# Attention into two expert layers on one core: the first set's tokens split by parity, items of two head pairs, and earlier loads

## The chip, the cores and the metric

One NeuronCore of one Trainium2 chip runs the whole program. The metric is the device time of one execution in microseconds. Five engines work side by side, each through its own queue in program order: TensorE (PE in the rows, its weight loads are PEld), VectorE (DVE), ScalarE (ACT), GpSimd (POOL) and SyncE (SP, which issues most of the DMAs).

## The reference

Three stages, all in float32. The tokens of all four sequences together are 2304, in rows of 512 features (8 heads of 64).

```python
# q, k, v: (4, 8, 576, 64); attention inside chunks of 64 tokens
scores = scale * q_c @ k_c.T            # per chunk and head
attn = softmax(scores)                  # sum + 1e-9 below the fraction line
x = (attn @ v_c) as rows (2304, 512)
p = domain_probs / (sum + 1e-9)         # 4 experts
x = sum over e of p[:, e] * (relu(x @ w1[e]) @ w2[e])      # 512 -> 1024 -> 512
h = x @ w_in                            # 512 -> 2048
out = (h * clip(h + 3, 0, 6) / 6) @ w_out                  # -> 512
```

## The kernel before

Every product of the two expert layers is made of three TensorE passes over a high and a low part of both operands (`HL`). The tokens are three sets of 768, each set two halves (z) of N = 384. The hidden features come in groups of 512: eight groups in phase 0 (4 experts), four in phase 1. Group 0 of a set is done plainly (`h_plain`, line 789). Every other group makes its four blocks of h from seven products of sums and differences of operands (`h_pair`, line 743), which `build_x` (lines 523 to 530) makes on ACT and DVE from the set's tokens. `y_unit` (line 836) multiplies the gated h by the second weight, and `finish` adds it up.

The order of work is written by a planner (`Plan`). Each piece of work is an `op` with an engine, an assumed duration, a due time, buffers and, for some, a time before which it may not start (`hold`). `Plan.run` plays them through once, in Python. `Plan.emit` then issues them in that order, and so each engine's queue has a fixed order on the chip. TensorE's products of the layers are the main list and keep their order. The attention's small TensorE steps are side work, put between them. While nothing is ready for TensorE early on, `fill` (line 249) issues a product of the identity with itself: one of 128 columns wherever the plan is between 3 and 40 us and sees TensorE free.

Set 0 is the start of the program. Its group 0 is cut into three parts of 256 tokens, and each part has two items (`Item`), an item being 128 tokens by all four head pairs. An item runs: load q, k, v (line 331, all from SP's queue, packets of 256 B), transpose q and k on TensorE (376), copy them out (480), scores (387), maximum, subtraction, exponential, sum and reciprocal (401 to 432), the weighing by it (436, on DVE in the first part and on POOL in the others), transpose the probabilities (440), copy (443), values (449), and two copies into the set's token tile `xs` (462). `build_plain` then makes the high part (559, ACT) and the low part (560, DVE) of the part's tokens, and `h_plain` of the part, 48 products of 256 columns, and its y, 24 products of 512 columns, can go. The two halves z are the first and the second 32 tokens of each chunk. Items of sets 1 and 2 are one head pair by 384 tokens and transpose on DVE (381).

The first group's weights come as one 1 MB load (`rh`, line 589). ACT casts each of its four quarters to the high part (582), POOL subtracts to the low part (583). They are also stored to DRAM for the later sets (`keep`, line 576). In SBUF, the identity (512 B a partition) stands ahead of the tile of all x operands (`x7`), then small constants and a pad, then the weight tiles `wh` and `wy` and the gated `gt`.

Of the kernel before, what the change touches and what calls it, by code (L numbers as in the profile page):

```python
# [21 lines left out]
PAD = 32  # L22
# [25 lines left out]
class Plan:  # L48
# [3 lines left out]
    LAT = 0.2  # L52

# [16 lines left out]
    def run(self):  # L70
# [51 lines left out]
        fillers = []  # L122

# [9 lines left out]
        while done < len(self.ops):  # L133
# [19 lines left out]
            for e in ready:  # L153
# [34 lines left out]
ANY = {"t", "a", "y", "h", "cm", "rh", "wp", "s", "w64", "tx"}  # L188
# [3 lines left out]
def fused_kernel(ctx: ExitStack, tc: tile.TileContext, q, k, v, probs, w1, w2, win, wout, out):  # L192
# [26 lines left out]
    x7 = const.tile([P, 7, 2, 2, N], F32R, name="x7")  # L219
# [4 lines left out]
    pn = const.tile([P, NT // P, NE], F32, name="pn")  # L224
    prs = const.tile([P, NT // P], F32, name="prs")

    const.tile([P, PAD], F32, name="pad")
    own = {tag: pool(tag, 1) for tag in ("wh", "wy", "gt")}
    sb = pool("sb", 1)
# [21 lines left out]
    plan = Plan({tag: n for tag, (n, _, _) in SHAPES.items()}, filler, 40.0)  # L251
# [85 lines left out]
    class Item:  # L337


        def __init__(self, si, ps, c0, n, by_pe=False, tags={}):  # L340
# [10 lines left out]
            self.xs = xs_of((0, si))  # L351

        def flat(self, b):
            return b.t.bitcast(F32).rearrange("p f w -> p (f w)") if b.tag in ("w64", "wp") else b.t
# [9 lines left out]
        def load(self, b, src, natural):  # L364
            if natural:
                h0 = 2 * self.ps[0]
                load_nat(self.nat(b), src, h0, h0 + 2 * len(self.ps), self.t0, self.n)
            else:
                w = 2 * self.nm
                t = b.t[:, :self.nc_ * 96].rearrange("p (c k) -> p c k", k=96)  # L370
                for i, p in enumerate(self.ps):
                    load_qk_t(t[:, i * w:(i + 1) * w], src, p, self.t0, self.n)

        def turn_pe(self, b, ps):
            for u in range(self.nu):
                nc.tensor.transpose(ps.t[:, u * P:(u + 1) * P], self.rows(b, u).rearrange("p h d -> p (h d)"), ident)  # L376

        def turn_dve(self, b, o, r):
            t = b.t[:, :self.nc_ * 96].rearrange("p (c k) -> p c k", k=96)
            d = o.t[:, :self.cols].rearrange("p (c i r) -> p c r i", c=self.nc_, r=2)  # L380
            nc.vector.transpose(out=d[:, :, r, :], in_=t[:, :, 64 * r:64 * r + 32])

        def scores(self):
            for c in range(self.nc_):
                for h in range(2):
# [3 lines left out]
                        self.flat(self.qT)[a, c * CH:(c + 1) * CH],  # L389
# [66 lines left out]
        def leave(self, c):  # L456
# [4 lines left out]
            d = d[:, 0] if len(self.ps) == 1 else d[:, :, 0]  # L461
            nc.scalar.copy(d, src)

        def place(self, t, step, quick=False, banks="aay"):
# [3 lines left out]
            ahead = 12.0  # L468
            by = self.by_pe
            for n_, (tag, src) in enumerate((("qr", q), ("kr", k), ("vr", v))):  # L470
                b, nat = getattr(self, tag), by or tag == "vr"
                kb = self.cols * P * 4 / 1000 * (1 if nat else 1.5)
                o[tag] = op("SP", 0.3, lambda b=b, src=src, nat=nat: self.load(b, src, nat), due(0 if n_ < 2 else 2) - ahead, new=[b], lag=kb / 200, hold=max(due(0) - 40, 0))
            for j, (a, z) in enumerate((("qr", "qT"), ("kr", "kT"))):
                src, dst = getattr(self, a), getattr(self, z)
                if by:
                    ps = buf("y")
                    x = op("PE", self.nu * 0.11, lambda src=src, ps=ps: self.turn_pe(src, ps), due(0), [o[a]], [ps], [src], side=True)
                    e_ = "ACT" if z == "qT" or not quick else "DVE"
                    f = (lambda dst=dst, ps=ps: nc.scalar.copy(self.flat(dst)[:, :self.cols], ps.t[:, :self.cols])) if e_ == "ACT" else (lambda dst=dst, ps=ps: nc.vector.tensor_copy(self.flat(dst)[:, :self.cols], ps.t[:, :self.cols]))  # L480
                    o[z] = op(e_, (act if e_ == "ACT" else dve)(self.cols), f, due(0), [x], [dst], [ps])
# [3 lines left out]
            self.psS, self.psP, self.px = buf(banks[0]), buf(banks[1]), [buf(banks[1]), buf(banks[2])]  # L485
            s = op("PE", self.nc_ * 0.036, self.scores, due(1), [o["qT"], o["kT"]], [self.psS, self.e], [self.qT, self.kT], side=True)
            if by:
# [8 lines left out]
            g = quick  # L496
            x = op("DVE" if g else "POOL", (dve if g else gps)(self.cols), lambda: self.weigh(nc.vector if g else nc.gpsimd), due(2) + 1, [x], (), [self.e, self.sm])
            x = op("PE", self.nu * 0.11, self.turn_p, due(3), [x], [self.psP, self.pT], [self.e], side=True)
            x = op("ACT", act(self.cols), self.copy_p, due(3), [x], (), [self.pT, self.psP])
            born = self.xs.born  # L500
            x = op("PE", self.nu * 0.22, self.values, due(4), [x, o["vr"], born], [*self.px, *([] if born else [self.xs])], [self.vr, self.pT, self.xs], side=True)
# [44 lines left out]
    def build_plain(key, c0, n, after, due):  # L546
# [3 lines left out]
        for d, z in [(d, zs) for zs in ((slice(0, 2),) if n < N else (slice(0, 1), slice(1, 2))) for d in range(2)]:  # L550
# [22 lines left out]
    def keep(ph, g, name, b, after, due):  # L573

        D = kept[ph, g, name] = dpool.tile([P, 2, 512], F32R, name=f"k{len(kept)}")
        stored[ph, g, name] = op("SP", 0.5, lambda: nc.sync.dma_start(out=raw(D), in_=raw(b.t)), due, after, (), [b], lag=1.75)

    def split_w(b, src, after, due, new, use, halves=True):
# [4 lines left out]
        return op("POOL", gps(512), lambda: nc.gpsimd.tensor_tensor(out=view(b.t[:, 1]), in0=read(), in1=raw(view(b.t[:, 0])), op=ALU.subtract), due, [hi, *after], (), [b, *use])  # L583
# [40 lines left out]
    def weights(ph, si, g):  # L624
# [17 lines left out]
        else:  # L642
            R, ld = load_h(ph, g, 1.0, 0)
            for d, f in ((0, 0), (1, 0), (0, 1), (1, 1)):
                b = wo[key, d, f] = buf("wh")
                x = wready[key, d, f] = split_w(b, lambda d=d, f=f: R.t[:, 2 * d:2 * d + 2, 256 * f:256 * f + 256], [ld], 6.0 + d + 2 * f, True, [R])
                keep(ph, g, (d, f), b, [x], 40)
        e, h = divmod(g, HS)
        for n_, f in enumerate(FO):
# [3 lines left out]
            ld = op("SP", 0.5, lambda Y=Y, r0=r0: nc.sync.dma_start(out=Y.t, in_=w2[e, r0:r0 + P, :]), (t_y - 8 if g else 2.0) + n_, (), [Y], lag=1.0, hold=hold_y)  # L653
            x = wready[key, "y", f] = split_w(b, lambda Y=Y: Y.t, [ld], t_y + 2 * n_, True, [Y], False)
            keep(ph, g, f, b, [x], t_y + 2 * n_ + 3)
# [121 lines left out]
    def h_plain(u, f, zs):  # L777
# [3 lines left out]
        ps = buf("h")  # L781
# [3 lines left out]
        def fn():  # L785
            for k_ in range(4):
# [7 lines left out]
        deps = [*(wready[key, d, f // 2] for d in range(2)), *(xplain[si, c0, d, z] for d in range(2) for z in zs)]  # L794
        x = op("PE", 12 * mm(m), fn, t, deps, [ps], [*Ws, *Xs])
# [49 lines left out]
    def out_rows(si, z, j):  # L845
        r0 = si * ST + 2 * P * j
        return out[r0:r0 + 2 * P, :].rearrange("(c z q) d -> z c q d", z=2, q=Q)[z]
# [59 lines left out]
    def domain_load():  # L907
        rows = probs.rearrange("(r c z q) e -> z c q r e", c=4, z=2, q=Q)
        d = pr.rearrange("p (r z) e -> p r z e", z=2)
        for z in range(2):  # L910
            for c in range(4):
                nc.sync.dma_start(out=d[32 * c:32 * c + 32, :, z, :], in_=rows[z, c])
# [11 lines left out]
    op("PE", 0.23, filler, 100, (), (), [warm], side=True, hold=40.3)  # L924

    SPARE = [{}, {"qr": "w64", "kr": "w64", "qT": "wp", "kT": "wp", "pT": "t"}]
    first_set = []
    for i in range(2 * N // PART):
        t = 3.0 + 11 * i
        after = []  # L930
# [81 lines left out]
```

## Time and profile before

| | |
|---|---|
| median of 3 runs | 1233.15 us (1231.62 to 1235.03) |
| the profiled execution | 1233.94 us, span 1232.2 us |
| mean granted TensorE clock | 0.997 |
| TensorE busy | 1213.1 us, 98% of the span |
| VectorE, ScalarE, GpSimd busy | 702.4, 515.1, 495.7 us |

The profiled execution lies 0.79 us above the median, and 1.74 us of it are outside the span. A busy TensorE includes products that only fill time (line 249) and products that run at the lower clock, so the 98% says little by itself about what could be saved. The rows below are of the profiled execution. Times in them are microseconds from the start of the span unless marked ns.

### The profile page before, as it was taken

The page shows a single profiled execution, that of the slowest core. Times are in us where ns is not written, and L with a number is a line of the kernel's source. Part 1 is how long each engine was busy: PE and PEld are TensorE (multiplying, and loading weights), DVE is VectorE, ACT ScalarE, POOL GpSimd, SP SyncE. Part 2 cuts the span into 40 slices and gives each one's busy share as a digit, 9 for nine tenths or more (in the row PEclk, how much of TensorE's full clock was granted, in tenths as well). Part 3 has the DMA queues.
Part 4 walks back from the last instruction along what each step waited for, and adds up shares of the span by engine and source line. Part 5 has one row for each costly group of instructions (what it writes and reads, how often), then busy time and mean ns, then how long its engine had stood idle before and what let it go on. Part 6 is the DMA issues. An engine that isn't in the chain of part 4 may idle for free.

```text
span 1232.2 us, 19532 instructions
## 1 busy us (share of the span) xinstructions
PE 1213.1 (98%) x7196; PEld 1090.1 (88%) x7196; DVE 702.4 (57%) x1267; ACT 515.1 (42%) x1149; POOL 495.7 (40%) x565
## 2 busy tenths in 40 slices
PE   9999999999999999999999999999999999999997
PEld 8888888888988888899998999998999999999996
DVE  4355645546634676557736655546455845584554
ACT  4554545454344455434453443324423442243221
POOL 3456655563244655455465574511111111111110
PEclk9999999999999999999999999999999999999999
DMA  8868877748679889878778878858555865675552
GB/s 241 283 223 290 275 233 264 254 191 284 209 211 316 264 269 281 273 267 262 223 258 273 288 269 293 300 188 259 186 185 186 269 205 188 188 239 188 188 171 52
DMA packets 150639, 292.32 MB, mean 237 GB/s; under 512 B 71056, under 2 KB 80528, under 8 KB 150160
## 3 DMA queue, kind: packets, MB, share of 16 engines
q0 software_dynamic: 43488, 158.35, 40.1%
q1 hardware_dynamic: 106864, 132.58, 33.2%
q8 instruction: 57, 0.93, 0.3%
q14 instruction: 38, 0.31, 0.1%
q10 hardware_dynamic: 192, 0.13, 0.0%
HBM read 213.95 MB, written 77.07 MB: 236 GB/s over the span
## 4 chain that ended last, share of the span: by engine, by line
PE 88%; POOL 3%; issue 3%; DMA 3%; SPq 2%; DVE 1%; ACT 1%; DVEq 0%; POOLq 0%; ACTq 0%
PE y L836 44%; PE h L743 35%; PE h L789 4%; PE y L249 1%; PE a L387 1%; SPq L324 1%; POOL wh L583 1%; DMA qr<-in_q_dram 1%; DMA rh<-in_moe_w_dram 1%; PE a L895 1%; PE a L449 1%; DMA w<-in_moe_w_in_dram 1%; POOL t L609 1%; PE y L376 0%; PE a L440 0%
## 5 line engine op out<-in xcount | busy, mean ns | idle before, releaser
L836 PE MATMUL y<-wy,gt 128*128 128x512 f32 x2592 | 606.6, 392 | 2.8 <-DVE gt L811 2.6
L836 PEld LDWEIGHTS y<-wy,gt 128*128 128x128 f32 x2592 | 484.3, 188 | 102.8 <-DVE gt L811 3.1
L743 PE MATMUL h<-x,wh 128*128 128x384 f32 x2772 | 500.1, 339 | 3.2 <-DVE c L753 1.6
L743 PEld LDWEIGHTS h<-x,wh 128*128 128x128 f32 x2772 | 485.6, 188 | 8.7 <-DVE c L753 3.2
L634 POOL DMA_DIRECT2D wh<-k x190 | 103.1, 543 | 210.0 <-PE h L743 198.9
L753 DVE TENSOR_TENSOR c<-h,c 128x384 f32<-128x384 f32 x264 | 145.8, 552 | 72.6 <-PE h L743 68.7
L637 POOL DMA_DIRECT2D wy<-k x112 | 61.6, 550 | 267.1 <-PE y L836 259.6
L863 DVE SCALAR_TENSOR_TENSOR acc<-y,pn,acc 128x512 f32<-128x512 f32 x126 | 88.6, 750 | 120.1 <-PE y L836 120.1
L753 DVE TENSOR_TENSOR c<-h,p 128x384 f32<-128x384 f32 x66 | 36.7, 556 | 137.2 <-PE h L743 118.2
L808 DVE TENSOR_TENSOR gt<-c,gt 128x384 fp32r<-128x384 f32 x126 | 97.4, 777 | 16.7 <-ACT gt L807 16.4
L760 ACT COPY p<-h 128x384 f32<-128x384 f32 x66 | 31.4, 476 | 175.1 <-PE h L743 175.1
L806 ACT ACTIVATE c<-c 128x384 f32<-128x384 f32 x126 | 65.5, 525 | 77.5 <-DVE c L753 77.2
L870 DVE TENSOR_TENSOR acc<-y,acc 128x512 f32<-128x512 f32 x53 | 36.3, 691 | 65.2 <-PE y L836 65.2
L807 ACT CAST gt<-c 128x384 fp32r<-128x384 f32 x126 | 64.1, 513 | 2.3
L817 ACT CAST gt<-t 128x384 fp32r<-128x384 f32 x96 | 47.0, 513 | 28.2 <-DVE t L816 28.2
L815 ACT ACTIVATE t<-c,half 128x384 f32<-128x384 f32 x72 | 43.0, 613 | 37.5 <-DVE c L753 37.5
L789 PE MATMUL h<-x,wh 128*128 128x384 f32 (+1 forms) x336 | 55.3, 318 | 0.8 <-DVE x L560 0.8
L583 POOL TENSOR_TENSOR wy<-t,wy 128x512 fp32r<-128x512 f32 x32 | 41.4, 1302 | 31.6 <-ACT wy L582 23.5
L789 PEld LDWEIGHTS h<-x,wh 128*128 128x128 f32 x336 | 51.1, 188 | 1.4 <-DVE x L560 1.0
L583 POOL TENSOR_TENSOR wp<-t,wp 128x512 fp32r<-128x512 f32 x32 | 41.9, 1308 | 22.5 <-ACT wp L582 22.1
L818 DVE TENSOR_TENSOR gt<-t,gt 128x384 fp32r<-128x384 f32 x96 | 49.9, 550 | 1.1
L583 POOL TENSOR_TENSOR wh<-t,wh 128x512 fp32r<-128x512 f32 x28 | 38.6, 1390 | 24.9 <-ACT wh L582 24.8
(113 smaller groups left out, 1011.5 us busy)
## 6 DMA issues: line engine op xcount, KB each, us to landing
wh<-k POOLq DMA_DIRECT2D x190, 512.0 KB, 6.1
wy<-k POOLq DMA_DIRECT2D x112, 512.0 KB, 4.6
k<-wh SPq DMA_DIRECT2D x53, 512.0 KB, 4.2
k<-wp SPq DMA_DIRECT2D x44, 512.0 KB, 5.4
k<-wy SPq DMA_DIRECT2D x32, 512.0 KB, 5.0
rh<-in_moe_w_dram SPq DMA_DIRECT2D x8, 1024.0 KB, 7.7
t<-in_moe_w_dram SPq DMA_DIRECT2D x32, 256.0 KB, 4.7
w<-in_moe_w_in_dram SPq DMA_DIRECT2D x16, 512.0 KB, 6.5
```

What stands on the lines that cost most here:

```text
L583: return op("POOL", gps(512), lambda: nc.gpsimd.tensor_tensor(out=view(b.t[:, 1]), in0=read(), in1=raw(view(b.t[:, 0])), op=ALU.subtract), ...
L634: wready[at_] = op("POOL", 0.6, lambda b=b, name=name: nc.gpsimd.dma_start(out=b.t, in_=kept[ph, g, name]), t - 14 + j, [stored[ph, g, nam ...
L637: wready[key, "y", f] = op("POOL", 0.6, lambda b=b, f=f: nc.gpsimd.dma_start(out=b.t, in_=kept[ph, g, f]), t_y - 6 + n_, [stored[ph, g, f] ...
L743: nc.tensor.matmul(acc.t[:, :n], W.t[:, a, k_ * 256 + pr_ * P:k_ * 256 + (pr_ + 1) * P], X.t[:, b, k_, cs], start=new and first, stop=last ...
L753: add = lambda out, x, y: (lambda: nc.vector.tensor_tensor(out=out(), in0=x(), in1=y(), op=ALU.add))
L789: nc.tensor.matmul(ps.t[:, :m], Ws[k_ // 2].t[:, a, k_ % 2 * 256 + f % 2 * P:k_ % 2 * 256 + f % 2 * P + P], x if len(zs) == 2 else x[:, zs ...
L806: x = op("ACT", act(n), lambda: nc.scalar.activation(src(), src(), AF.Relu), due, after, (), bufs)
L807: hi = op("ACT", act(n), lambda: nc.scalar.copy(hi_(), src()), due + 0.1, [x], [G], bufs)
L808: lo = op("DVE", dve(n) * busy(ph), lambda: nc.vector.tensor_tensor(out=lo_(), in0=src(), in1=raw(hi_()), op=ALU.subtract), due + 0.3, [hi ...
L818: lo = op("DVE", dve(n), lambda: nc.vector.tensor_tensor(out=lo_(), in0=r_(), in1=raw(hi_()), op=ALU.subtract), due + 0.9, [hi], (), [G, R])
L836: nc.tensor.matmul(ps[j].t, G.t[:, a, o + j * P:o + (j + 1) * P], W.t[:, b, :], start=f == FO[0] and i == 0, stop=f == FO[-1] and i == len ...
L863: fn = lambda: nc.vector.scalar_tensor_tensor(out=A.t, in0=ps.t, scalar=p, in1=A.t, op0=ALU.mult, op1=ALU.add)
```

## The change

- **Halves.** z is now the parity of the token. q and k of two neighbouring tokens land on one partition in one packet of 512 B. A new step `sort` brings them by parity (a copy of 512 columns: ACT for q and DVE for k in the first part, POOL for both in the others), and TensorE's transposes write their results with a step of two columns (k) or by halves of chunks (q).
- **Items.** An item is now 256 tokens by two head pairs; a part still has two. The second item of each part does its exponentials on ACT, chunk by chunk with sums (`exp_sums`), the first on DVE and ACT as before. `build_plain` is called for each item, for its half of the features. The first part's `h_plain` is cut in two: the first half of the features for all four blocks, then the second half into the same four PSUM banks.
- **Loads.** The first part's k goes out from ACT's queue, and so does the first w1 load, now as two halves. The later parts load into buffers of their own (`wh`, `acc`), with holds of 3 and 8 us in the plan. The stores of the first weights are held to 38 us. The probabilities come in one DMA where eight were.
- **Fillers.** At most one per 0.6 us of the plan, from 1.5 to 24 us.
- **Addresses.** The pad goes, two small tiles move behind, and `x7`, `wh`, `wy`, `gt` begin at multiples of 1 KB.

```diff
-PAD = 32
+Y0 = 18.0
+LOADS = (((0.0, 0.0, 1.0), (0.4, 0.4, 1.5)), ((3.0, 3.0, 4.0), (3.1, 3.1, 4.1)), ((8.0, 8.0, 10.0), (8.1, 8.1, 10.1)))
+BANKS = (("hhhh", "hhhh"), ("aaay", "yyay"), ("aaay", "aaay"))
+    EVERY = 0.6
...
-                    if e == "PE" and 3.0 < now < self.warm:
+                    if e == "PE" and filled < now < self.warm:
                         fill(now)
+                        filled = now + self.EVERY
...
+                    queue.dma_start(
+                        out=self.flat(b)[off // 2:(off + m) // 2, :self.cols].rearrange("p (h k) -> p h k", k=2 * D),
+                        in_=src[b_, h0:h1, s_:s_ + m, :].rearrange("h (p e) d -> p h (e d)", e=2),
+                    )
...
+        def sort(self, eng, b):
+            i = self.flat(b)[:, :self.cols].rearrange("p (h e d) -> p e h d", e=2, d=D)
+            o = self.sorted_(b)[:, :self.cols].rearrange("p (e h d) -> p e h d", e=2, d=D)
+            (eng.copy if eng is nc.scalar else eng.tensor_copy)(o, i)
...
+                o = o.rearrange("p (t e) -> p e t", e=2) if b is self.kr else o.rearrange("p (c e q) -> p e c q", e=2, q=Q)
...
-            R, ld = load_h(ph, g, 1.0, 0)
+                lds.append(op("ACT", 0.6, lambda d=d, src=src: nc.scalar.dma_start(out=R.t[:, 2 * d:2 * d + 2], in_=src), 1.0 + d, (), () if d else [R], [R], lag=2.0))
...
-            it = Item(0, list(range(NP)), PART * i + P * m, P, by_pe=True, tags=SPARE[m])
-            after += it.place(t, 3.0, quick=i == 0, banks="aay" if i else "hhh")
+            it = Item(0, [2 * m, 2 * m + 1], PART * i, PART, by_pe=True, tags=HERE[2 * i + m])
+                on_act=m == 1, weigh_on="DVE" if not i else "POOL", queues=("SP", "ACT", "SP") if not i else ("SP", "SP", "SP"),
+                sort_on=("ACT", "DVE") if not i else ("POOL", "POOL"),
...
+                firsts = [h_plain(u, f, (0, 1), range(2), None) for f in range(GF)]
+                for f in range(GF):
+                    h_plain(u, f, (0, 1), range(2, 4), firsts[f])
```

## Rows read from the trace of the kernel before

**Rows 1.** The page's first part: busy time, share of the span, instructions.
```profile
PE 1213.1 (98%) x7196; PEld 1090.1 (88%) x7196; DVE 702.4 (57%) x1267; ACT 515.1 (42%) x1149; POOL 495.7 (40%) x565
```
**Rows 2.** Stretches: length, busy PE, PEld, DVE, ACT, POOL, granted clock, DMA share, GB/s.
```profile
0.00:31.40 31.40, 29.61 (x380) 28.10 (x381) 15.79 (x30) 14.03 (x26) 12.08 (x15) 1.00 0.88 244
31.40:82.30 50.90, 46.17 (x448) 40.09 (x447) 23.80 (x42) 27.36 (x54) 19.93 (x17) 0.97 0.73 224
...
75.00:80.00 5.00, 3.90 (x12) 3.10 (x13) 2.88 (x7) 1.92 (x3) 1.52 (x1) 0.75 0.97 222
```
**Rows 3.** The chain up to 31.4 us: shares; start, length, what.
```profile
by line: PE y L249 53.2%; PE y L376 14.2%; DMA qr<-in_q_dram 9.7%; PE a L387 6.8%; PE h L387 6.8%; PE h L449 4.0%; PE h L440 2.8%; issue 0.4%
...
0.75 3.07 DMA qr<-in_q_dram
...
29.23 2.32 PE y L249 x19
```
**Rows 4.** The chain behind 31.4 us, and one piece of it much later.
```profile
31.66 2.85 PE h L789 x24
...
76.10 6.23 PE y L836 x19
...
82.33 14.74 PE h L743 x84
...
707.70 16.34 PE y L836 x72
```
**Rows 5.** TensorE's groups from 31.4 to 82.3 us: busy, mean ns, idle before.
```profile
L836 PE MATMUL y<-wy,gt 128*128 128x512 f32 x72 | 20.0, 427 | 2.6 <-DVE gt L811 2.6
L789 PE MATMUL h<-x,wh 128*128 128x256 f32 x144 | 19.3, 287 | 0.8 <-DVE x L560 0.8
```
**Rows 6.** The order of time, steps of the first part: start, length, what.
```profile
8.04 1.15 PE L387 MATMUL h<-kT,qT 64*64 64x64 f32 x32
...
9.23 0.69 DVE L401 TENSOR_REDUCE st<-h 128x8 f32<-128x512 f32 x1 [1.73 <-PE h L387]
...
10.68 0.63 ACT L426 ACTIVATE e<-e 128x512 f32<-128x512 f32 x1 [1.95 <-DVE e L422]
...
13.79 0.68 DVE L436 TENSOR_TENSOR e<-e,st 128x512 f32<-128x512 f32 x1
...
15.84 0.60 PE L440 MATMUL h<-ident,e 128*128 128x128 f32 x4
...
20.17 0.69 PE L449 MATMUL h<-pT,vr 64*64 64x64 f32 x32
...
20.91 0.65 ACT L462 COPY xs<-h 128x256 f32<-128x256 f32 x2 [2.29 <-PE h L449]
...
27.33 1.14 ACT L559 CAST x<-xs 128x512 fp32r<-128x512 f32 x2
...
27.98 1.29 DVE L560 TENSOR_TENSOR x<-xs,x 128x512 fp32r<-128x512 f32 x2 [0.29 <-ACT x L559]
```
**Rows 7.** DMA packets of the first 60 us.
```profile
DMA packets 27384, 16.08 MB, mean 268 GB/s; under 512 B 23792, under 2 KB 23792, under 8 KB 27376
```
**Rows 8.** The order of time: first weights, probabilities, first stores, one chunk's exponential.
```profile
11.02 7.13 SPq L912 DMA_DIRECT2D pr<-in_moe_domain_probs_dram  x8
...
13.56 2.18 ACT L582 CAST wh<-rh 128x512 fp32r<-128x512 f32 x4 [2.25 <-DMA rh<-in_moe_w_dram]
...
14.26 5.05 POOL L583 TENSOR_TENSOR wh<-rh,wh 128x512 fp32r<-128x512 f32 x4 [12.95 <-ACT wh L582]
...
20.40 1.28 SPq L576 DMA_DIRECT2D k<-wh  x2
...
102.23 0.31 ACT L411 ACTIVATE e<-a,st 128x64 f32<-128x64 f32 x1 [2.51 <-DVE st L406]
```
**Rows 9.** The order of time: last copies of the third and the sixth item.
```profile
37.74 0.38 ACT L462 COPY xs<-y 128x256 f32<-128x256 f32 x1
...
63.91 0.38 ACT L462 COPY xs<-y 128x256 f32<-128x256 f32 x1
```

More of the change, by code (lines that the diff above doesn't have):

```diff
@@ L249, in filler @@
         nc.tensor.matmul(warm.t[:, :P], ident, ident, start=True, stop=True)
-    plan = Plan({tag: n for tag, (n, _, _) in SHAPES.items()}, filler, 40.0)
+    plan = Plan({tag: n for tag, (n, _, _) in SHAPES.items()}, filler, 24.0)
     op = plan.op
@@ L460, in leave, with place @@
             d = self.xs.t[:, ps].rearrange("p k z (m c q) -> p c k m z q", c=2, q=Q)[:, c, :, m0:m0 + self.nm]
-            d = d[:, 0] if len(self.ps) == 1 else d[:, :, 0]
-            nc.scalar.copy(d, src)
-        def place(self, t, step, quick=False, banks="aay"):
+            if len(self.ps) == 1:
+                nc.scalar.copy(d[:, 0], src)
+            else:
+                src = src.rearrange("p (i m) z q -> p i m z q", m=self.nm)
+                for i in range(len(self.ps)):
+                    nc.scalar.copy(d[:, i], src[:, i])
+        def place(self, t, step, banks="aaay", loads=(), k_on="ACT", on_act=True, weigh_on="POOL", queues=("SP", "SP", "SP"), s_hold=0.0, sort_on=("ACT", "DVE")):
             o = {}
             due = lambda j: t + j * step
-            ahead = 12.0
             by = self.by_pe
@@ L472, in place @@
                 kb = self.cols * P * 4 / 1000 * (1 if nat else 1.5)
-                o[tag] = op("SP", 0.3, lambda b=b, src=src, nat=nat: self.load(b, src, nat), due(0 if n_ < 2 else 2) - ahead, new=[b], lag=kb / 200, hold=max(due(0) - 40, 0))
+                on = queues[n_]
+                queue = nc.sync if on == "SP" else nc.scalar
+                when = loads[n_] if loads else due(0 if n_ < 2 else 2) - 12.0
+                o[tag] = op(on, 0.5 if n_ < 2 else 1.0, lambda b=b, src=src, nat=nat, queue=queue: self.load(b, src, nat, queue), when, new=[b], lag=kb / (230 if by and n_ < 2 else 122 if by else 200), hold=max(when if loads else due(0) - 40, 0))
             for j, (a, z) in enumerate((("qr", "qT"), ("kr", "kT"))):
@@ L582, in split_w @@
         hi = op("ACT", act(512), lambda: nc.scalar.copy(view(b.t[:, 0]), read()), due, after, [b] if new else (), [b, *use])
-        return op("POOL", gps(512), lambda: nc.gpsimd.tensor_tensor(out=view(b.t[:, 1]), in0=read(), in1=raw(view(b.t[:, 0])), op=ALU.subtract), due, [hi, *after], (), [b, *use])
+        return op("POOL", gps(512), lambda: nc.gpsimd.tensor_tensor(out=view(b.t[:, 1]), in0=read(), in1=raw(view(b.t[:, 0])), op=ALU.subtract), due, [hi, *after], (), [b, *use], hold=hold)
     def load_h(ph, g, due, hold):
@@ L785, in fn @@
         def fn():
[L786 removed]
+            for k_ in ks:
                 for i, (a, b) in enumerate(HL):
@@ L907, in domain_load @@
     def domain_load():
[L908 to L912, printed above, removed]
+        nc.sync.dma_start(out=pr.rearrange("p (r z) e -> p r (z e)", z=2), in_=probs.rearrange("(r p z) e -> p r (z e)", p=P, z=2))
     def domain():
```

135 lines of the change are left out of this document (82 added, 53 removed), and 3 rows, old and new, of the table HERE.

## The prediction

> **What bounds the kernel now.** The page's first part comes first: TensorE is busy 98% of the span [rows 1]. So time can come back only where its busy time is not the layers' work. The stretches and the chain say where that is. Up to 31.4 us TensorE shows 29.61 us of busy time [rows 2], but 53.2% of the chain there, 16.7 us, is line 249, the filler, which computes nothing [rows 3]. The fillers stand in TensorE's queue between the steps of the first two items. Where the chip is ahead of the plan they are the delay: the last run of them, 19 products and 2.32 us, ends where the first real product starts [rows 3], while the part's first low half took 1.29 us for both features' halves from 27.98 [rows 6] and so was there at 29.3.
>
> From 31.4 to 82.3 us the three parts of group 0 run: 144 products of 256 columns and 72 of 512 [rows 5]. Undisturbed, 24 of the first take 2.85 us (118.8 ns each) and 72 of the second 16.34 us (226.9 ns each) [rows 4], so the three parts need 17.1 + 16.3 = 33.4 us. The stretch has 50.9 us. Of the 17.5 us over, 4.7 are idle (50.9 less 46.17 busy [rows 2]), 1.9 are the lower clock near 75 us (19 products took 6.23 us where 4.31 were due [rows 4], and the granted clock of 75 to 80 us is 0.75, a mean of the two levels [rows 2]), and the other 10.9 are the later items' small steps. The first seven-product group starts at 82.33 us [rows 4]. Behind that the engine is steady, and nothing in the change's text touches what runs there but addresses and the order of the halves. So I ask: when will that group start, and do the addresses change the price of a product?
>
> **The first product of the layers.** I put its start at 20 us, where it is 31.4. The chain of the first item, step by step: q alone lands 3.07 us after its issue at 0.75 [rows 3]; k now goes out at the same moment from ACT's queue, 512 KB in all, and at the mean 268 GB/s [rows 7] the second 256 KB is 1 us more, so both are there at about 4.8. Then the sort (new; nearest rows a DVE pass of 512 columns in SBUF, 0.68, and an ACT one, 0.63 [rows 6]) 0.65; eight transposes 1.3 (four take 0.60 [rows 6], the first of them at the lower clock); copy out 0.69 like the other DVE reads of PSUM; scores 1.15; maximum, subtraction and sum 3 x 0.69, exponential 0.63, two small ones 0.4; weighing 0.68; transposes 0.60; copy 0.6; values 0.69; four copies of 128 columns, at most 0.33 each (two of 256 took 0.65), 1.3; high part 0.57 and low part 0.65 (half of 1.14 and of 1.29) [rows 6]. That is 12.0 us. Some 15 hand-offs of 0.1 make 1.5. The second item shares DVE and ACT: its k sort and its maximum with the bias (0.65 + 0.9) and its first exponentials may stand ahead, 1.5 us. 4.8 + 12.0 + 1.5 + 1.5 = 19.8.
>
> What else must be there is earlier: w1 is landed at 13.56 now and split by POOL at 14.26 + 5.05 = 19.3 [rows 8], and its halves now leave in the first microseconds, behind 1.5 MB at most of other loads instead of behind 1.5 MB and SP's issue of them. SP's queue also loses the 7.13 us that issuing the eight small DMAs of the probabilities held it [rows 8], behind which the second part's loads waited, and the stores of 20.40 us [rows 8] go behind the loads. Their readers are the sets to come, hundreds of microseconds later. The four issues on ACT's queue (about 0.5 us each in SP's rows: 1.28 for two [rows 8]) stand ahead of the first sort, which waits for data until 4.8 anyway.
>
> The first half of the features alone can start TensorE, but its four blocks hold four PSUM banks, and the second item's scores, probabilities and values want the same four. So I give the split no more than the 11.4 us (31.4 less 20), and bound it from below by 8 (the second item's end, some 3 us later, counts) and from above by 14 (no sharing of engines, hand-offs hidden).
>
> **Given back later.** Some small steps that ran before 31.4 now run behind the first product: two scores of the second part at 1.15, eight transposes of four at 0.44 to 0.60, and the second item's tail of 1.3, less what the second part will have done by 20: I take 4 us (2 to 6). The second and third part's loads no longer wait for buffers or stores; the idle 4.7 us I take as 3, a return of 1.7 (0 to 4.7). The k transposes write PSUM at every second column. No row shows that; the bounds are nothing and a doubling of 0.15 us for each of 24, of which 16 fall behind the first product, 2.4 us; I take 0.3, as nearly all of it lies beside ACT's and DVE's chains. (The Trainium skill, "PSUM — Partial Sum Buffer", Specifications, has 8-byte lines there and says that any non-contiguous pattern slows matmuls significantly; by that the doubling would be the better guess, and the sum 2.1 us worse. No run here shows it.) For the sorts of the later parts POOL gets eight passes at 1.26 (5.05 for four [rows 8]), 10.1 us on top of 12.08 + 19.93 [rows 2]: 42 of some 73 us. They are hidden beside TensorE's 33.4 us as long as they come ahead of the weights' splits in POOL's queue. Behind a sort the item's transposes wait, and TensorE's queue with them. ACT gets three times eight exponentials at 0.31 [rows 8] for one of 0.63 (5.6 us), two sorts (1.3) and twelve more copies (at most 3.9): 41.4 busy [rows 2] becomes 52 of 73.
>
> Together: 11.4 - 4.0 + 1.7 - 0.3 = 8.8 us. The group of line 743 would start at 73.5.
>
> **The addresses.** The rows give the overhead of a product over its columns at 2.4 GHz: 84 of 384 columns took 14.74 us [rows 4], 175.5 ns, 15.5 over 160.0; 512 columns 13.6 over 213.3; 256 columns 12.1 over 106.7. All three read tiles off 1 KB today, and yet differ by at most 3.4 ns. If the start address were in that, the most to gain is 3.4 ns on each of 2772 + 192 products of 384 columns, 10.1 us; the most to lose, 512 columns becoming as dear as 384, 1.9 x 2592 = 4.9 us. Nothing in the rows speaks for either: 512 columns stream a weight tile behind odd-sized small tiles and are no dearer than the 384 that stream `x7`, which starts at a multiple of 512 B. I take nothing. (The Trainium skill, "SBUF — State Buffer", Specifications (TRN2), has lines of 16 bytes, so tiles at multiples of 64 B would already be whole; by that also nothing. The trace can't tell.)
>
> **Sum.** 1233.15 - 8.8 = 1224.35, say 1224.3. For its own execution that is 1233.94 - 8.8 = 1225.1, a span of 1223.4.
>
> **The rivals.**
> *Nothing but the start moves.* The four later items go through a single PSUM bank for scores, probabilities and half of the values. In the trace the third item's last copy is at 37.74 and the sixth's at 63.91 [rows 9]: 8.7 us an item. If they keep that pace and each gains a sort of 1.26, 10.0, then from an end of the second item at 23 the sixth is done at 63, where it is now, the last part's products start with it, and only the idle time near 75 us can come back: 2 to 5 us, 1230. For it: ACT and POOL get more work. Against it: today's loads of these items wait for buffers, and TensorE is busy 46 of 50.9 us there, so the pace may be TensorE's.
> *Addresses help.* All of the 10.1 us: 1214. For it speaks only the spread of 3.4 ns.
> *The lower clock: slower.* With one filler per 0.6 us of the plan TensorE has less to do before 20 us and between items. If it stays at 1.2 GHz through the first part, that part's third of the 33.4 us and its 3 us of small steps take 14 us more: 1238. It decides from 8.8 us of work done at half speed; beyond 12.5 the kernel is slower than can be mistaken. For it: idle of 2.6 us [rows 5] was enough near 75 us. Against it: that cost 1.9 us, and the engine was back within the 19 products [rows 4].
> *The change does not reach the end.* The start is earlier, but the groups behind 82 us wait longer for weights or tokens: 1233. Against it: the products of line 743 run at their steady price right from 82.33 [rows 4].
>
> **How the numbers follow.** My forecast 0.55, with 1219 to 1229 as its own range (gain of 4 to 14 us from the bounds above); only the start 0.16; addresses 0.13; lower clock 0.09; nothing reaches the end 0.07. About 0.3%, 3.7 us, is what can be told from no change here, so faster begins below 1229.5. Faster: nearly all of the forecast (0.53), addresses 0.13, half of "only the start" 0.08: 0.74. Same: the other half, the last rival and 0.01: 0.16. Slower: the clock's and 0.01 from the last: 0.10. The range 1214 to 1232 leaves out the clock's case, most of the last, and what of the addresses' case goes below 1214.
>
> **What would show it.** Right: line 249 under 5 us of the chain; the first row of line 789 near 20 us; the first of line 743 near 73; 14.74 us still for 84 of its products. Wrong: a first 789 later than 25, waits of TensorE for ACT or POOL between 25 and 75 us, a granted clock under 1 behind 10 us, or another price of a product late in the span, which would outweigh all the rest.

## The result and the profile after

The changed kernel takes 1212.92 us (median of 5, 1211.53 to 1213.66) where the kernel before took 1233.31 beside it (5, 1231.62 to 1235.03): a ratio of 0.9826 [0.9815, 0.9838], 20.4 us less. The forecast was 1224.3, its range began at 1214. The profiled execution took 1213.07 us, its span is 1211.3, 20.9 less than before. One execution of run (a) below, 1897.5 us at a granted clock of 0.58, is in no number.

The page's first part, to be held against [rows 1]:

```profile
span 1211.3 us, 19404 instructions
PE 1196.7 (99%) x7096; PEld 1074.0 (89%) x7096; DVE 704.9 (58%) x1265; ACT 521.1 (43%) x1209; POOL 498.6 (41%) x573
```

TensorE runs 100 products fewer and is busy 16.4 us less; all 100 are fillers (52 in all where there were 152). The rest of the gain is idle time. Where the two lie is told by the first start of each product line. h of group 0 is now line 839, the seven products are line 792, the filler 256, y 888; after each line name stand count, shortest, median and longest duration in ns, first and last start in us (the last one is the seven products of the kernel before):

```profile
L839 PE MATMUL h<-x,wh x336: 274/334/426, 23.3 to 595.2; 128*128 128x384 f32 x96, 128*128 128x256 f32 x72
...
L792 PE MATMUL h<-x,wh x2772: 331/334/446, 69.3 to 1187.0; 128*128 128x384 f32 x198
```

```profile
L743 PE MATMUL h<-x,wh x2772: 331/337/449, 82.2 to 1207.7; 128*128 128x384 f32 x198
```

The first product of the layers starts at 23.3 us instead of 31.4 (8.1 earlier), the first group of seven products at 69.3 instead of 82.2 (12.9 earlier). Behind that group the program is shorter by another 8.0. (A second run of the same program, the last experiment, has 22.5 and 68.5: these places are good to some 0.8 us.) The windows split at the same places as [rows 2], and the rest (length, then busy PE, PEld, DVE, ACT, POOL):

```profile
0.00:23.30 23.30, 19.59 (x250) 17.80 (x251) 8.29 (x20) 13.36 (x39) 8.27 (x14) 1.00 0.97 262
23.30:69.40 46.10, 45.25 (x478) 39.91 (x477) 26.48 (x50) 34.36 (x103) 28.12 (x25) 1.00 0.71 245
...
69.40:1211.30 1141.90, 1131.91 (x6373) 1016.27 (x6371) 670.09 (x1196) 473.39 (x1070) 462.17 (x536) 1.00 0.74 241
```

The kernel before, behind its own group, same columns:

```profile
82.30:1232.20 1149.90, 1137.28 (x6373) 1021.87 (x6371) 662.84 (x1196) 473.69 (x1069) 463.65 (x535) 1.00 0.73 238
```

Both run the same 6373 products there. They are busy 5.4 us less, and idle 10.0 us instead of 12.6. So the 20.9 us are: 8.1 up to the first product, 4.8 from there to the group, 5.4 less busy time behind it, 2.6 less idle time there. Most of the 5.4 is the price of a product. It is seen in the chain late in the span (start, length, what), to be read against [rows 4]:

```profile
705.37 14.58 PE h L792 x84
719.96 16.36 PE y L888 x72
```

84 products of 384 columns take 14.58 us where they took 14.74: 173.6 ns each instead of 175.5. 33 such groups make 5.3 us. The 72 of 512 columns take 0.02 us more than before (16.34), 0.7 us over 36 groups.

### The profile page after: what moved, and what is told of

The parts are those of the page before. It is cut to its first block, busy times and chain, and to the rows that moved or that the text cites. A ratio compares the mean times of both kernels' runs of the same rounds, so it can differ in the third digit from the quotient of the medians.

```text
span 1211.3 us, 19404 instructions
## 1 busy us (share of the span) xinstructions
PE 1196.7 (99%) x7096; PEld 1074.0 (89%) x7096; DVE 704.9 (58%) x1265; ACT 521.1 (43%) x1209; POOL 498.6 (41%) x573
## 4 chain that ended last, share of the span: by engine, by line
PE 93%; issue 2%; POOL 1%; DMA 1%; DVE 1%; ACT 1%; SPq 1%; DVEq 0%; POOLq 0%
PE y L888 46%; PE h L792 38%; PE h L839 4%; PE a L423 1%; PE a L485 1%; PE a L947 1%; DMA w<-in_moe_w_in_dram 1%; PE a L476 1%; PE y L406 0%; SPq L331 0%; DVE c L802 0%; DMA kr<-in_k_dram 0%; DMA qr<-in_q_dram 0%; PE y L256 0%; POOL wh L627 0%
## 5 line engine op out<-in xcount | busy, mean ns | idle before, releaser
L792 PE MATMUL h<-x,wh 128*128 128x384 f32 x2772 | 494.7, 336 | 1.7 <-DVE c L802 1.1
L802 DVE TENSOR_TENSOR c<-h,c 128x384 f32<-128x384 f32 x264 | 146.0, 553 | 71.6 <-PE h L792 68.5
L860 DVE TENSOR_TENSOR gt<-c,gt 128x384 fp32r<-128x384 f32 x126 | 100.4, 803 | 12.5 <-ACT gt L859 12.1
L447 ACT ACTIVATE e<-a,st 128x64 f32<-128x64 f32 x104 | 31.0, 318 | 42.3 <-DVE st L442 35.1
```

Of the source, the lines that this page charges most:

```text
L792: nc.tensor.matmul(acc.t[:, :n], W.t[:, a, k_ * 256 + pr_ * P:k_ * 256 + (pr_ + 1) * P], X.t[:, b, k_, cs], start=new and first, stop=last ...
L802: add = lambda out, x, y: (lambda: nc.vector.tensor_tensor(out=out(), in0=x(), in1=y(), op=ALU.add))
L860: lo = op("DVE", dve(n) * busy(ph), lambda: nc.vector.tensor_tensor(out=lo_(), in0=src(), in1=raw(hi_()), op=ALU.subtract), due + 0.3, [hi ...
```

## The experiments

All are timed beside the kernel before on the same chip, where it took 1233.3 to 1234.5 us; ratios are to it. The change was timed again beside only the last of them, so differences to its 1212.92 are good to about 1 us. "Group" is the first start of the seven-product line (69.3 in the change, 82.2 before).

### Addresses

The program as compiled has the old `x7` at 640 bytes past a multiple of 1 KB, so 128 past one of 256, and the old `wh`, `wy`, `gt` at 512 past 1 KB. In the change all four are at multiples of 1 KB.

**Only x7 back to its old offset; only x7 moved in the kernel before.**

```diff
 # the change, x7 640 bytes on
+    const.tile([P, 160], F32, name="shift")
     x7 = ...
+    const.tile([P, 96], F32, name="rest")
 # the kernel before: x7 allocated behind pr, at a multiple of 1 KB
-    x7 = const.tile([P, 7, 2, 2, N], F32R, name="x7")
     pr = ...
+    x7 = const.tile([P, 7, 2, 2, N], F32R, name="x7")
```

> The changed kernel, its x operands alone shifted to where they started before (640 bytes past a multiple of 1 KB, 128 past one of 512); order and every other tile as in the change. Theory 1, the start of the moving x operand sets the price of a 384-column product: 84 of them take 14.74 us again (175.5 ns each), the group of line 792 still starts near 69.4 us, and the time is 1212.9 + 2964 x 1.9 ns = 1218.5 us. Theory 2, the weights' addresses did it: 14.58 us stays and the time is 1213. Theory 3, the price fell for some other reason (order of the work): 14.58 us and 1213 too.

> The kernel before, with the x operands alone moved to a multiple of 1 KB (their tile is allocated behind the small constants; the weight tiles stay where they were). Theory 1: 84 products of 384 columns take 14.58 us, the time falls by 5.6 us to 1227.7. Theories 2 and 3: 14.74 us stays, 1233.3.

Measured: 1216.43 us (0.986 [0.9845, 0.9874]), 3.5 above the change; and 1229.96 (0.9969 [0.9959, 0.998]), 3.7 below the kernel before (1233.69 beside it). The chain late in the span, first of the change with `x7` back, then of the kernel before with `x7` moved:

```profile
706.36 14.74 PE h L794 x84
```

```profile
720.71 14.59 PE h L743 x84
```

The price goes with the address of `x7` alone, both ways. The group's start moves by 0.5 and 1.1 us (68.8 and 81.1). The whole gives less than the 5.6 us that both expectations had: behind the group TensorE is busy 4.1 us more than in the change in the first run, and 4.9 less than before in the second, in part since the 512-column products go the other way by 0.7. (The profiled execution of the second took 1228.62, 1.3 below its median.) In every run of this section that edits the change, each engine's queue holds the same order of work as in the change, so the addresses are all that differs.

**Which distance?** `x7` by 512, then by 256 bytes; the weights and `gt` by 128; all four by 128; `gt` alone by 128.

```diff
 # 512: [P, 128] ahead of x7, [P, 128] behind; 256: [P, 64] and [P, 192]
 # weights and gt by 128: [P, 32] behind x7; all four: [P, 32] ahead of x7
+    const.tile([P, 32], F32, name="shift")
 # gt alone
-    own = {tag: pool(tag, 1) for tag in ("wh", "wy", "gt")}
+    own = {tag: pool(tag, 1) for tag in ("wh", "wy")}
+    shift = pool("shift", 1)
+    shift.tile([P, 32], F32, name="shift")
+    own["gt"] = pool("gt", 1)
```

> The changed kernel, with the x operands at 512 bytes past a multiple of 1 KB. If what matters is a multiple of 512 bytes: 14.58 us for 84 products and 1213. If it has to be 1 KB: the price rises for one half of the operands, those whose start now leaves 1 KB, but as each operand is 1536 bytes long half of them left it already, so again about 1213; only a rule on the tile's own start would give 14.74 us and 1218.5.

> The changed kernel, x operands 256 bytes past a multiple of 512, weights at a multiple. If the distance of the two operands counts in steps of 512: 84 products of 384 columns take 14.74 us. If in steps of 256: 14.58.

> The changed kernel, with the x operands at 1 KB but the tiles of both weights and of the gated h shifted by 128 bytes. These are the stationary operand of the 384-column products, and both operands of the 512-column products. Theory 1 in its wide form, any moving operand off a multiple of 512 bytes costs: 72 products of 512 columns go from 16.36 us to about 16.50 and the time to 1212.9 + 2592 x 1.9 ns = 1217.8, while the 384-column products keep 14.58. Theory 2: the 384-column products rise to 14.74 and the time to 1218.5. If the price belongs to the x tile alone, nothing moves: 1213.

> The changed kernel with both the x operands and the tiles of the weights and of the gated h 128 bytes past a multiple of 512. If each operand has to start at a multiple of 512 by itself: 84 products take 14.74 us and the time is 1216.4, as when one of them was shifted. If it is the distance between the two operands that counts: 14.58 us and 1213.

> The changed kernel with only the gated h (stationary in line 888) shifted by 128 bytes, its weights (moving, 512 columns), x and the first weights at multiples of 1 KB. If the distance of moving and stationary operand counts for every product: 72 products of 512 columns go from 16.36 us to some 16.50 (1.9 ns each), time 1217. If it is only so for 384 columns, where the moving operand ends off a multiple of 1 KB: 16.36 us, time 1213.

Measured: `x7` by 512 1214.01 us (0.9837 [0.9822, 0.9852]); by 256 1211.55 (one execution); weights and `gt` by 128 1216.14 (0.9856 [0.9842, 0.9871]); all four by 128 1212.23 (0.9829 [0.9814, 0.9844]); `gt` alone 1223.89 (one execution). With `x7` moved by 512 or 256 the 84 products take 14.59 and 14.58 us. The chains late in the span of the other three, in this order:

```profile
738.37 14.74 PE h L793 x84
753.11 16.34 PE y L889 x72
```

```profile
704.52 14.58 PE h L793 x84
719.10 16.36 PE y L889 x72
```

```profile
710.36 14.59 PE h L795 x84
724.95 16.73 PE y L891 x72
```

A tile's own address doesn't matter: all four 128 bytes off are as cheap as none. What matters here is how far the streamed operand and the weight operand lie apart, modulo 256 bytes. 128 apart costs 1.9 ns on a product of 384 columns (`x7` against `wh`), and 5 ns (232.4 for 227.2) on one of 512 (`gt` against `wy`), more than the 1.9 that was expected. In the first of these chains the 512 columns stay cheap since `wy` and `gt` moved together. Only distances of 0 and 128 modulo 256 were run.

### Fillers

**The old rule in the change, the new rule in the kernel before, none in the change.**

```diff
 # old rule (the change): at every free moment from 3 to 40 us of the plan
-                    if e == "PE" and filled < now < self.warm:
+                    if e == "PE" and 3.0 < now < self.warm:
-    plan = Plan(..., filler, 24.0)
+    plan = Plan(..., filler, 40.0)
 # new rule (the kernel before): the reverse; none (the change): 24.0 -> 0.0
```

> The changed kernel with the fillers of before: one wherever the plan sees TensorE free between 3 and 40 us. Theory 1, the fillers in TensorE's queue were the delay of the start: the first product of the layers goes from 23.3 to 28 or later, the group of line 792 from 69.3 to 74 or later, and the time to about 1217. Rival, the fillers only fill time in which TensorE would wait for the same data: the first product stays within 1 us of 23.3, the time at 1213.

> The kernel before with the fillers of the change: at most one per 0.6 us of the plan from 1.5 to 24 us. Theory 1: the first product of line 789 goes from 31.4 to 27 or earlier and the time falls by 3 us or more, to 1230 or less. Rival, loads and items set the start: 31.4 stays within 1 us and the time at 1233.

> The changed kernel with no fillers behind the first two. Theory 1, the fillers are a cost in TensorE's queue and little else: the first product at 23 or earlier, time 1213 or less. Rival, the fillers hold the granted clock: without them the first products run at the lower clock (24 products of 256 columns in more than 4 us instead of 2.9) and small steps before it, the group of line 792 starts 2 us later or more, time 1215 or more.

Measured: old rule in the change 1229.39 us (0.9954 [0.9938, 0.9971]), first product at 24.6, group at 72.7. New rule in the kernel before 1225.43 (0.9936 [0.9921, 0.9951]), first product 27.2, group 78.1. None 1221.66 (0.9901 [0.9886, 0.9915]), first product 28.3, group 75.9.

So the sparser fillers alone give the kernel before 8.5 us (1233.9 beside it), 4.1 of it at the group, all of that already at the first product. The rest is behind the group, where TensorE idles 9.5 us instead of 12.6 (length, then busy PE):

```profile
78.10:1223.90 1145.80, 1136.29 (x6373) 1022.61 (x6371) 660.25 (x1196) 473.31 (x1070) 462.46 (x536) 1.00 0.73 238
```

Up to the group its chain then holds long pieces of loads:

```profile
6.15 7.72 DMA rh<-in_moe_w_dram
...
28.86 9.30 DMA kr<-in_k_dram
```

Without fillers (six at the very start stay) the first product comes 5.0 us later and the group 6.6. Two things are in that, and the run does not part them. One is order: played through without fillers, the plan puts DVE's sort of the second item's k behind the first item's sum, where it also takes 1.32 us for 0.42. DVE in the change, then without fillers, then TensorE's transposes of it without fillers (order of time):

```profile
11.94 0.42 DVE L396 COPY w<-w 128x512 f32<-128x512 f32 x1
```

```profile
14.73 1.32 DVE L396 COPY w<-w 128x512 f32<-128x512 f32 x1
```

```profile
16.20 1.09 PE L406 MATMUL y<-ident,w 128*128 128x128 f32 x4 [4.65 <-DVE w L396]
```

These transposes are 3.6 us later than the change's (12.57, shown further down), though the first item was no later (its sum starts at 12.74 where the change's starts at 13.03). The other is the lower clock, in the 1.4 us that come on top up to the first product: the four transposes take 1.09 us where the change's take 0.60, the second item's scores 1.60 for 1.15. A window of it (the seventh value behind the length is the granted clock):

```profile
20.00:30.00 10.00, 6.95 (x113) 6.38 (x104) 3.94 (x9) 7.76 (x32) 0.00 (x0) 0.83 0.88 195
```

So the rival of the lower clock is there, but as the smaller part, and its 24 products in more than 4 us did not come.

The old rule costs the change 1.3 us at the first product, 3.4 at the group, and 16.5 in all; neither expectation has that. Up to 32 us only the fillers differ, behind that the order of the queues too. Most of the 16.5 is lost far behind the last filler (43.3 us): the named waits of TensorE there are 11.4 us where the change has 2.3. The longest, in order of time at 702 us, DVE, then POOL, then TensorE:

```profile
702.97 8.07 DVE L860 TENSOR_TENSOR gt<-c,gt 128x384 fp32r<-128x384 f32 x2
```

```profile
702.67 1.31 POOL L653 TENSOR_TENSOR t<-rh 128x512 f32<-128x512 f32 x1
...
708.89 1.25 POOL L653 TENSOR_TENSOR t<-rh,t 128x512 f32<-128x512 f32 x1
```

```profile
710.62 0.80 PE L888 MATMUL y<-wy,gt 128*128 128x512 f32 x1 [3.82 <-DVE gt L860]
```

Two DVE steps that read two tiles in SBUF take 8.07 us while POOL runs six two-operand steps back to back, and TensorE waits. Over the whole run the same line against one whose input h is in PSUM (shortest, median, longest in ns):

```profile
L860 DVE TENSOR_TENSOR gt<-c,gt x126: 517/552/7595, 79.7 to 834.5; 128x384 fp32r<-128x384 f32 x126
...
L863 DVE SCALAR_TENSOR_TENSOR gt<-h,gt x70: 414/550/560, 30.1 to 831.4; 128x384 fp32r<-128x384 f32 x58, 128x256 fp32r<-128x256 f32 x12
```

The plan has one order for the whole program. An edit at its start moves what meets what hundreds of microseconds later: with the new fillers in the kernel before, the queues' order of work differs at places up to 615 us; with the old ones in the change, up to 766.

**Sparse fillers and the moved x7 in the kernel before.**

> The kernel before with the x operands moved to a multiple of 1 KB and the fillers of the change. If the two parts add up: 1233.5 - 3.7 - 8.3 = 1221.5, the group of line 746 or so starting at 78 and 84 products at 14.58 us. Rival, part of what the fillers gave was later order and takes another turn with other addresses: 1224 or more.

Measured: 1222.26 us (0.9898 [0.9869, 0.9927]), group 76.2. The two gains alone, 8.5 and 3.7, add up to 1221.1 from 1233.3, within the interval. That is 11.1 us, more than half of the change's gain, without its new items or loads. Behind its group this run is as short as the change (1141.9):

```profile
76.20:1217.50 1141.30, 1131.88 (x6373) 1016.81 (x6372) 658.10 (x1196) 473.37 (x1070) 463.72 (x536) 1.00 0.74 239
```

So in these traces what the new items and loads add lies ahead of the group: 6.9 us (76.2 to 69.3). By the medians it is 9.3, as the profiled execution here (1219.25) was 3.0 below its median. How much of it is the items and how much the loads, no run shows.

### Loads, buffers, stores

```diff
 # a: k and the w1 halves from SP's queue
-    queues=("SP", "ACT", "SP") if not i else ...
+    queues=("SP", "SP", "SP") if not i else ...
 # b: LOADS for the first part alone
-    loads=LOADS[i][m]
+    loads=LOADS[0][m] if not i else ()
 # c: no hold on the stores of the first weights
-                keep(ph, g, (d, f), b, [x], 40, 38)
+                keep(ph, g, (d, f), b, [x], 40)
-            keep(ph, g, f, b, [x], t_y + 2 * n_ + 3, 0 if g else 38)
+            keep(ph, g, f, b, [x], t_y + 2 * n_ + 3)
 # d: all parts in the first part's two buffers
-        {"vr": "acc"}, {"qr": "w64", ...},
-    )
+    ) * 3
```

> The changed kernel with the first part's k and both halves of w1 issued from SP's queue like all other loads. Theory 1, the second queue saves only the time of issue, some 1 to 3 us on k and w1: the first product of the layers goes from 23.3 to 24 or 26, and the time to 1213 to 1215. Rival, w1 behind all of the first part's loads is late and holds TensorE: the first product after 27, the time 1216 or more.

> The changed kernel, with the loads of the second and third part due and held as before (12 us ahead of their items in the plan's order, instead of from 3 and 8 us). Theory 1, early loads are what lets the small steps of these parts run without waits: from the first product of the layers to the group of line 792 it takes 48 us or more where it is 46.0, TensorE waits for DMA in there, and the time is 1215 or more. Rival, the loads are hidden either way: 46.0 and 1213.

> The changed kernel, with the stores of the first group's weights no longer held to 38 us of the plan. Theory 1, the stores take DMA time and SP's queue from the loads of the later parts: the group of line 792 starts later than 69.3, at 71 or more, time 1215. Rival: the loads were all issued before the stores come, nothing moves, 1213.

> The changed kernel, its later parts' loads into the same buffers as the first part's (as before the change) instead of buffers of their own. Theory 1, waiting for buffers is what made the later parts late: the loads of the third part are issued only when the second part is through its transposes, TensorE waits for them, and the group of line 792 starts at 74 or later instead of 69.3, time 1218 or more. Rival, the buffers are free early enough since the loads are ahead in SP's queue anyway: 69 to 71, time 1213 to 1215.

(a) 1216.55 us (three executions; 0.9863 [0.9847, 0.988]): as neither expectation had it, the first product is a little earlier, at 22.9, but the group at 71.1. Its window from 10 to 20 us has the lower clock in it (0.77):

```profile
10.00:20.00 10.00, 6.80 (x93) 6.16 (x89) 4.63 (x9) 6.84 (x27) 6.56 (x7) 0.77 0.99 291
```

That did not make the first product late. Between it and the group TensorE waits 0.8 us, as in the change, but does more small steps that the change had behind it by then: 128 scores for 96, 24 transposes of q and k for 19. The order of the queues is another one here too.

(b) 1233.8 us (1.0001 [0.9992, 1.001]), first product 38.0, group 83.3. The edit did not do what its expectation says. Without times of their own the later parts' loads became due ahead of the first part's. SP's queue:

```profile
0.75 0.45 SPq L377 DMA_DIRECT2D wh<-in_q_dram  x1
...
13.72 0.48 SPq L377 DMA_DIRECT2D qr<-in_q_dram  x1
```

The first part's q goes out at 13.72 us. So it says nothing on own times for the later loads, but it prices their order, with the lower clock that came along (0.71 from 20 to 30 us): 13 us of q's issue are 14.7 us of the first product, and 14.0 at the group.

(c) 1221.71 us (0.99 [0.9885, 0.9915]), first product 23.0, group 74.1. The group is as late as Theory 1 had it, but not by late transfers: TensorE waits for none in that stretch. With the early stores the queues have another order, and DVE's steps take twice as long beside POOL's as alone (order of time, DVE, then POOL):

```profile
58.84 1.93 DVE L574 TENSOR_TENSOR xs<-xs 128x768 f32<-128x768 f32 x1
...
61.56 0.94 DVE L574 TENSOR_TENSOR xs<-xs 128x768 f32<-128x768 f32 x1
```

```profile
54.29 5.67 POOL L627 TENSOR_TENSOR wh<-t,wh 128x512 fp32r<-128x512 f32 x3
```

TensorE then waits 2.8 us for DVE's gated h, and the lower clock takes 1.9 more, as it did near 75 us before (19 products in 6.22 us for 4.31; the wait, then the chain). Together these are nearly all of the 4.8 us at the group:

```profile
PE y L888 <- DVE gt L863: 2.8, 1, 2.8
```

```profile
68.01 6.22 PE y L888 x19
```

(d) 1242.75 us (1.0071 [1.0045, 1.0097]), slower than the kernel before: first product at 26.8, group at 75.8, 6.5 later, and some 23 us more behind it. These are the numbers of Theory 1, but not its way: between the two TensorE waits 1.3 us, none of it for a load. As without fillers, DVE's sort of the second item's k stands behind the first item's sum, and TensorE waits 3.7 us for it. Of the two longest waits behind the group, one (3.8 us, for line 860) is of the kind of 702 us above. The other is longer, and there ACT had waited for a load (the wait, then ACT in order of time):

```profile
PE y L888 <- ACT gt L862: 6.7, 1, 6.7
```

```profile
303.14 0.66 ACT L718 ACTIVATE t<-w 128x512 f32<-128x512 f32 x1 [10.58 <-DMA w<-in_moe_w_in_dram]
```

### The split of the first part

```diff
-                for zs in (...) if n_ else ():
+                for zs in (...) if n_ else ((0, 1),):
-            if not n_:
+            if False:
```

> The changed kernel, with the first part's products in one piece, which wait for both items. Theory 1, the split only moves 2.9 us of products ahead of the second item's end: the first product goes from 23.3 to 25 or 26, the group of line 792 from 69.3 to between 70 and 72, time 1214 to 1215.5. Rival, TensorE has other small steps to do there: nothing moves, 1213.

> The changed kernel with the first part's products in one piece and the x operands 256 bytes past a multiple of 512: the two runs that came out below the change, together. If both were real: 1211 or a little less, 1 to 2 us below the changed kernel of the same job. Rival, they were within the noise of one job: no difference beyond 1 us.

> The changed kernel as it is, beside the run before it on the same chip: 1212.9 within 1 us, the group of line 792 at 69.3, 84 products in 14.58 us, and the same waits of TensorE behind 70 us (the order is fixed).

Measured: unsplit 1211.59 us (0.982 [0.9803, 0.9836]), first product 24.7, group 68.1. Unsplit with `x7` 256 bytes on 1211.58 (0.9819 [0.9801, 0.9836]); the change again beside it 1212.41 (0.9822 [0.9806, 0.9837]). The change's second run has 22.5 and 68.5 (69.3 was expected), the last unsplit one 25.1 and 68.5. So the split brings the first product 1.4 to 2.6 us forward and the group not at all, against the expected 1 to 3 us. It gains nothing, and no version here beats the change by more than the measurement can tell.

## Why the prediction was right and wrong

Direction and place of the first gain were right; the size was not: 20.4 us for 8.8. Two steps failed, and two terms were mis-sized. Of the 12.1 us of span that the sum missed, 5.4 are busy time behind the group, 2.6 idle time there, and 4.1 the group's start (12.9 earlier for 8.8).

**The addresses failed.** "I take nothing" rested on "`x7`, which starts at a multiple of 512 B" and "nothing in the rows speaks for either". `x7` started 128 past a multiple of 256, which stands in no row, and the step compared starts of single tiles where the distance between two operands counts. The 5.4 us of busy time lie inside the bound of 10.1; moved alone, `x7` is worth 3.5 to 3.7 us of time. The rival asked for 3.4 ns a product; 1.9 were there. The rule of 16-byte lines (the Trainium skill, "SBUF — State Buffer", Specifications (TRN2)), by which also nothing, doesn't cover it: every address run here is a multiple of 16 bytes, and the price moved.

**"Behind that the engine is steady" failed.** Its idle time there fell from 12.6 us to 10.0. The named waits of the two kernels behind their groups, TensorE's (in total, times, longest), the change first:

```profile
PE h L792 <- DVE c L802: 1.1, 2, 0.8
PE y L888 <- ACT xs L498: 0.6, 1, 0.6
PE h L792 <- ACT p L809: 0.6, 1, 0.6
```

```profile
PE h L743 <- DVE c L753: 1.6, 3, 1.1
PE h L743 <- DVE gt L811: 1.6, 1, 1.6
PE a L387 <- ACT xs L462: 1.4, 1, 1.4
```

These are 2.3 and, with one more of 0.2, 4.8 us. The sentence allowed the order of the halves to matter there and then gave it no price and no bound; the old fillers in the change lose 13 us there, shared buffers 23. It also took the rest of the order for untouched, but the plan is played through anew. In the kernel before, the new fillers alone bring the idle time there from 12.6 us to 9.5 (9.4 with `x7` moved too), so the 2.6 can come without any new item or load; within the change itself it was not taken apart.

**The first product: mis-sized, 23.3 for 20.** Its chain, as [rows 3], and the scores in the chain of the second run:

```profile
by line: DMA kr<-in_k_dram 17.7%; PE y L406 16.5%; PE y L256 13.8%; PE h L423 13.0%; ACT e L447 10.2%; PE h L476 5.3%; PE a L423 4.4%; DVE e L472 3.5%; ACT wp L409 2.5%; ACT pT L479 2.5%; PE h L485 2.2%; DVE t L396 1.9%; issue 1.8%; DVE st 
...
0.74 4.15 DMA kr<-in_k_dram
...
5.40 1.12 PE y L406 x4
...
8.65 1.90 PE h L423 x32
...
16.21 2.39 ACT e L447 x16
```

```profile
7.50 1.17 PE h L423 x32
```

k landed at 4.9 as the step had it (4.8). The fillers still hold 13.8% of the 23.5 us, 3.2 us, a little under the 5 that were to show it right; the step gave them no time at all. The scores took 1.90 at the lower clock for 1.15. That is in part the execution's luck: in the second run of the change they took 1.17, and its first product came at 22.5. And the chain goes through the second item's eight exponentials and the eight readings of their sums, 2.39 us, where the sum gave all of that item 1.5: the step named this sharing, and its lower bound (8 us) is what came.

**Given back later: wrong in sign.** It priced 4.0 us of small steps coming behind the first product, less 1.7 us of idle. From first product to group the stretch fell by 4.8, to 46.1. Idle there is 0.85, not 3; the 1.9 us at the lower clock near 75 us are gone; and what is left is 11.8 (45.25 less 33.4), only 0.9 above the 10.9 of before. The 10.9 were not all small steps, as the prediction read them: 1.1 us are fillers, which ran on to 47.8 us (0.4 in the change), so the small steps grew by 1.6, not 4.0. The POOL sorts, put at 1.26 each from a two-operand step, take 0.57 (order of time, then the transposes of q and k):

```profile
17.17 2.28 POOL L396 COPY wh<-wh 128x512 f32<-128x512 f32 x4
```

```profile
11.24 0.60 PE L406 MATMUL y<-ident,w 128*128 128x128 f32 x4
...
12.57 0.60 PE L406 MATMUL y<-ident,w 128*128 128x128 f32 x4
```

The second four are k's, written at every second column. They cost what q's cost, and what four cost before [rows 6]. The rule that any non-contiguous pattern slows a matmul (the Trainium skill, "PSUM — Partial Sum Buffer", Specifications (TRN2)), by which the sum was to be 2.1 us worse, is not borne out for these writes.

**The rivals.** Only the start moves: no, the later items kept up with TensorE, which idles 0.85 us of the 46.1. Addresses help: yes, and its 1214 (the forecast less 10.1) came nearest to the 1212.9, but partly by luck: about half of its 10.1 came, and the earlier group and the idle time made up the rest. The lower clock: in the change only up to the first scores; it is a part of what the run without fillers loses, and it stands ahead of the first product in runs (a) and (b). The change doesn't reach the end: the reverse.

## What to carry to other kernels

Put the streamed and the weight operand of a product a multiple of 256 bytes apart in SBUF (128 past that was the dear case here), and read it off one group of back-to-back products late in the span: a few ns each is a term of the sum when thousands follow. Fillers cost on both sides, too many by delaying the queue, none by the lower clock. Where an order is planned as a whole, every edit of the plan's input also changes the order, so compare the queues' orders before putting a difference down to the edit's own effect; such an edit can move later stalls by more than it moves the start, and a prediction needs a bound for that.

## What the runs showed that was not expected

- 128 bytes (modulo 256) between the operands cost 1.9 ns on 384 columns and 5 ns on 512. Those of 256 columns don't show it: 24 took 2.85 us before [rows 4], 2.88 in the unsplit run.
- A DVE step with two inputs in SBUF, 0.55 us by the median, took 7.6 us beside back-to-back two-operand steps of POOL, much longer than one of these (1.25 to 1.31). Another, with an input in PSUM, never took over 0.56.
- A granted clock of 1.00 in a window near the start can mean that nothing was recorded yet. In the run without fillers the window from 10 to 20 us reads 1.00, while its four transposes at 16.20 take 1.09 us for 0.60. The trace's first record of a granted clock begins at 19.3 us there (at 10.95 in the change, 5.8 before), and a stretch without a record counts as 1.00. The durations show the lower clock.
